# Rows of h computed during the last attention steps, and their six weights converted with fewer VectorE steps

## The chip, the cores and the metric

The kernel runs on one core of a Trainium2 chip. The metric is the device time of one launch in microseconds, the median of several runs.

## The reference, cut to what matters

```python
# q, k, v: [2, 8, 768, 64]; proj: [64, 6]; all float32
q_bits = einsum(q, proj) > 0 ; k_bits = einsum(k, proj) > 0       # 6 bits each
mask   = q_bucket[..., :, None] == k_bucket[..., None, :]
scores = where(mask, q @ k.T / sqrt(64), -1e9)
attn   = softmax(scores); x = (attn @ v) -> [1536, 512]
h = max(x @ w1, x @ w2, x @ w3)            # w: [512, 768]
y = h @ w_out                              # [768, 512]
u = y @ w_in                               # [512, 2048]
out = (u * clip(u + 3, 0, 6) / 6) @ w_out2 # [2048, 512]
```

All products keep float32 accuracy: an operand is split into a rounded high part and a low part, and a product is made of three matmuls (high by high, high by low, low by high). The host passes the weights as one int64 tensor of 56 blocks of 128 x 512 (`wts`), and the core turns each block back into a high and a low tile.

## The kernel before

The order of every engine is written out by hand (`tc.manual_schedule()`): an engine's queue holds instructions in the order in which the Python code issues them, and numbers at the top of the file say at which step a piece is issued.

**Attention** (`attention`, L237) has 16 heads in 8 pairs `p`. A prologue (`prologue`, L624) loads and splits the first pair, computes the bucket bits of head 0 (`bits_mm`, `bits_cmp`) and runs the six row-maximum units of head 0 (`max_unit`, L494 on TensorE, L498 on VectorE). Bits of the pair's second head go through a tile `bt` (`bits_bt`, L393) and two DMAs into the operand tiles (`bits_out`). Then 96 steps follow, six to a head, and six more (`LAG`) that only finish. In step `s` the program issues:

1. the product with V of step `s - 6` (`pv`, L578 to L584: 18 + 2 short matmuls), into the one PSUM buffer `x` of three steps; the division `norm` (L590, L595, L598: VectorE, tiles `xd`, `xr`, `xo`) must have read `x` before the next three steps write it;
2. the scores (`scores`, L544, four matmuls into one of two buffers `s`), and on ScalarE two exponentials of them, `E` (L548) and, in 16 bits, `ph` (L551); in some steps VectorE makes `ph` from `E` instead (L561; `PH_DVE`, and `PH_TAIL` from step `TAIL` on);
3. the low part `pl` (L566) of the step before, on GpSimd or, where `PL_DVE` or `PL_TAIL` says so, on VectorE;
4. a row-maximum unit for a step ten ahead (`mu`), and the tasks set for this step with `at` and `po`: loads, splits, bits of a later pair (`bits`, 12 matmuls), `vabs` to `vmean` for V, `fin` (L606, L607: transposes of the result, copied to `xF`), and the split of `x` of the first batch (`xhi` L199 on ScalarE, `xlo` L202 on VectorE, at the steps `XH`).

Three PSUM buffers with the tag `m` serve row maxima, bits, `fin`, `vsum` and `vmean` in turn.

**Weights** come by `job(i)` (L140), a generator that `tick` advances. It loads a block (`wraw`, 512 KB), scales half of it on ScalarE into `wy` (L146), takes three bits of the other half (`wr`: on VectorE for the first six blocks, L149; on GpSimd later, L155), joins them with two VectorE instructions (L160, L163), and writes the high tile `wh` on ScalarE (L169) and the low one `wl` on GpSimd (L171). In the attention `tick` is called after each step from `JS + 1` on, and starts jobs `JG` (in the tail `JT`) ticks apart, six in all (`J0`).

**The rows of h** (`hunit(ft, b, ..)`, L209) for a column tile `ft` (of 6) and a batch `b` (of 2) take 72 matmuls of 128 x 384: three weights by four blocks of x by three products by two halves (`mm`, L108). The unit (0, 0) is a generator `hu`: from step `HU0 = 92` on, each step issues six of its matmuls, and the rest goes between the last `fin` tasks. The other eleven units follow in `moe` (L764) one after the other, (1, 0) first; then come `w_out`, `w_in`, the gate and `w_out2`. `moe` splits x of the second batch at its start (`xsplit`, L205), while (1, 0) runs. Tiles that `moe` uses lie in memory that the attention has given up; the unit (0, 0) uses tiles `T` of the attention that are free by then.

## Time and profile before

| | us |
|---|---|
| median of 3 runs (lowest to highest) | 721.07 (720.88 to 722.88) |
| the profiled execution | 721.92 |
| span of the profiled execution, first to last instruction | 720.1 |
| TensorE matmul busy / weight load busy | 695.7 / 645.0 |
| VectorE / GpSimd / ScalarE busy | 456.7 / 395.6 / 337.0 |

The page has the busy time of each engine, the span in 40 slices (busy share in tenths, and the TensorE clock that was granted), and the chain of work that ended last. That chain is TensorE for 80% of the span and VectorE for 14%. Steps 0 to 95 can be told apart in the timeline by the first score matmul of each (L544, `s<-QB,KB`): step 0 begins at 18.1 us, step 12 at 58.6, step 72 at 192.3, step 88 at 228.9, step 95 at 246.0. `moe` begins at 263.3 us with (1, 0), and (0, 1) follows at 275.8.

### The profile page before, as it was taken

How to read it: one execution, taken by the hardware profiler on the slowest of the kernel's cores; microseconds unless marked ns; L12 is line 12 of the kernel's file. 1: busy time of each engine (PE TensorE's matmuls, PEld its weight loads, DVE VectorE, ACT ScalarE, POOL GpSimd, SP SyncE). 2: the span in 40 equal slices, each digit the busy share in tenths (PEclk: the TensorE clock that was granted, in tenths of full speed). 3: DMA queues.
4: the chain of work that ended last, by engine and by line, in shares of the span. 5: the costliest groups of instructions: out<-in, count | busy, mean ns of one | idle time of the engine just before them, and what ended most of it. 6: DMA issues, size and time to landing. Idle time of an engine off the chain costs nothing.

```text
span 720.1 us, 13570 instructions
## 1 busy us (share of the span) xinstructions
PE 695.7 (97%) x5343; PEld 645.0 (90%) x5343; DVE 456.7 (63%) x848; ACT 337.0 (47%) x564; POOL 395.6 (55%) x290
## 2 busy tenths in 40 slices
...
GB/s 179 108 163 125 110 190 139 116 163 169 107 121 56 35 59 60 88 88 89 30 59 89 60 30 58 59 87 64 115 66 80 92 26 62 86 30 1 1 77 99
DMA packets 22528, 61.82 MB, mean 86 GB/s; under 512 B 3864, under 2 KB 4952, under 8 KB 22464
## 3 DMA queue, kind: packets, MB, share of 16 engines
...
q8 instruction: 42, 0.69, 0.4%
...
q14 instruction: 22, 0.18, 0.1%
...
## 4 chain that ended last, share of the span: by engine, by line
PE 80%; DVE 14%; ACT 3%; issue 2%; DMA 1%; SPq 1%; DVEq 0%; ACTq 0%
PE s L108 28%; PE m L108 25%; PE s L544 7%; PE x L108 7%; PE m L494 4%; DVE mx L498 2%; PE x L578 2%; DVE G L788 2%; PE x L579 2%; PE x L580 2%; DVE wy L160 1%; DVE wy L163 1%; DVE pl L566 1%; DVE g L791 1%; ACT gr L782 1%
## 5 line engine op out<-in xcount | busy, mean ns | idle before, releaser
L155 POOL TENSOR_SCALAR wr<-wraw 128x256 int32<-128x256 uint32 x100 | 127.0, 1270 | 139.1 <-DVE wy L160 103.3
L566 POOL TENSOR_TENSOR pl<-E,ph 128x768 f16<-128x768 f32 x83 | 150.1, 1820 | 38.6 <-ACT ph L551 18.3
L498 DVE TENSOR_REDUCE mx<-m 128x1 f32<-128x384 f32 x192 | 97.0, 547 | 23.1 <-PE m L494 21.0
L548 ACT ACTIVATE E<-s 128x768 f32<-128x768 f32 x96 | 77.8, 810 | 55.9 <-PE s L544 47.2
L171 POOL TENSOR_TENSOR wl<-wy,wh 128x512 fp32r<-128x512 f32 x48 | 74.2, 1546 | 45.2 <-ACT wh L169 42.7
L108 PE MATMUL s<-G,wh 128*128 128x384 f32 x360 | 76.9, 334 | 0.0
L788 DVE TENSOR_TENSOR G<-g,G 128x384 fp32r<-128x384 f32 x56 | 45.0, 845 | 49.9 <-ACT G L787 49.4
L578 PEld LDWEIGHTS <-ph 128*128 128x128 f16 x576 | 54.8, 99 | 21.0 <-DVE xo L598 11.2
L578 PE MATMUL x<-VV,ph 128*128 128x65 f16 x576 | 65.8, 197 | 7.4 <-DVE xo L598 7.2
L169 ACT ACTIVATE wh<-wy 128x512 fp32r<-128x512 f32 x48 | 30.3, 631 | 75.5 <-DVE wy L163 75.5
L494 PE MATMUL m<-T,T 76*128 76x384 f32 x192 | 56.4, 366 | 9.5 <-DVE mx L498 4.6
L579 PE MATMUL x<-VV,ph 128*128 128x65 f16 x576 | 65.3, 197 | 0.0
L580 PE MATMUL x<-VV,pl 128*128 128x65 f16 x576 | 64.9, 194 | 0.0
L551 ACT ACTIVATE ph<-s 128x768 f16<-128x768 f32 x79 | 63.8, 808 | 0.0
L108 PEld LDWEIGHTS s<-G,wh 128*128 128x128 f32 x360 | 63.7, 188 | 0.0
L544 PE MATMUL s<-QB,KB 128*128 128x384 f32 x192 | 59.2, 391 | 0.8 <-ACT ph L551 0.8
L160 DVE SCALAR_TENSOR_TENSOR wy<-wy,wr 128x512 int32<-128x512 int32 x56 | 43.5, 778 | 25.1 <-POOL wr L155 25.0
L146 ACT ACTIVATE wy<-wraw 128x512 f32<-128x512 f32 x56 | 37.7, 672 | 45.5 <-POOL wl L171 27.5
L108 PE MATMUL m<-T,wh 128*128 128x384 f32 x240 | 58.6, 337 | 0.0
L579 PEld LDWEIGHTS <-ph 128*128 128x128 f16 x576 | 55.2, 99 | 0.6 <-issue 0.6
L108 PE MATMUL m<-G,wh 128*128 128x384 f32 x216 | 55.8, 334 | 0.0
L163 DVE SCALAR_TENSOR_TENSOR wy<-wraw,wy 128x512 int32<-128x512 int32 x56 | 54.3, 970 | 1.9
(209 smaller groups left out, 1682.5 us busy)
## 6 DMA issues: line engine op xcount, KB each, us to landing
...
```

Of the source, the lines that this page charges most:

```text
L108: pe.matmul(u[0:m, 0:n], l, r[:, hf * n:(hf + 1) * n], start=(first and i == 0), stop=(last and i == len(pairs) - 1),)
L155: pool.tensor_scalar(out=r3[:, c], in0=raw[:, c, 0].bitcast(U32), scalar1=2.0 ** -29, scalar2=7.0, op0=ALU.mult, op1=ALU.min,)
L171: pool.tensor_tensor(out=wl, in0=f32(y), in1=f32(wh), op=ALU.subtract)
L494: pe.matmul(u[:, 0:HF], QA[h % NA][0:76, qt * 128:qt * 128 + 128], KA[h % NA][0:76, hsl(hf)], start=True, stop=True,)
L498: dve.tensor_reduce(out=mx[h][:, qt, hf:hf + 1], in_=u[:, 0:HF], axis=AX.X, op=ALU.max)
L544: pe.matmul(u[:, k, 0:HF], a[0:n, c], b[0:n, hsl(hf)], start=n == 128, stop=n < 128)
L548: act.activation(out=e, in_=u[:, :, 0:HF], func=AF.Exp, scale=BIG)
L551: act.activation(out=ph.rearrange("p (a b) -> p a b", a=2), in_=u[:, :, 0:HF], func=AF.Exp, scale=BIG,)
L566: eng.tensor_tensor(out=pl, in0=e, in1=ph, op=ALU.subtract)
L578: pe.matmul(o, ph[:, c], vv[:, 0:65], start=kt == 0, stop=False)
L579: pe.matmul(o, ph[:, c], vv[:, 65:130], start=False, stop=False)
L580: pe.matmul(o, pl[:, c], vv[:, 0:65], start=False, stop=False)
```

## The change

- **h.** The units (0, 0) and (1, 0) are both issued in the attention, by a new generator `hfill`: per weight and half 12 matmuls into one `m` buffer, three of them to a call of `next` (48 calls in all). From step 88 on, each step makes two calls (six matmuls); six calls go ahead of each `fin` that is left after the last step, and two remain for the end. The running maximum goes to two new tiles `hF`, and `hsplit` splits them in `moe`, which starts with (0, 1).
- **x of the first batch** is split earlier, at steps 40, 49, 61, 69 (before: 81, 86, 89, 92), into tiles of its own.
- **The six early weights** start at steps 39, 45, 51, 57, 63, 69 (before: 63, 72, 81, 90, 94, 98). ScalarE, not VectorE, now makes `wr`, and the scaled half lies in a PSUM buffer `m` (`y0`), not in `wy`, until the two VectorE instructions have joined the parts.
- **Bits** of the second head (`bits_bt`, `bits_out`) are issued ahead of head 0's maxima. Numbers that place other tasks change too: row maxima of heads 1 and 2 (`MU`), loads into `KB` and `QB` (`AL`), `vabs`, `vmean`, the first `fin` of a pair; `TAIL` is 88, and in the tail ScalarE makes `ph` in three of six steps (before: in one). The prologue's warm-up matmuls are fewer, and the first six steps get some (`WS`).

```diff
-WARM = (9, 4, 4, 2)
-TAIL = 85
+WARM = (9, 4, 3, 1)
+TAIL = 88
+B0 = 0
+F0 = 2
+WS = (4, 0, 4, 2, 2, 2)
-PH_TAIL = (1, 2, 3, 4, 5)
+PH_TAIL = (1, 4, 3, 4, 3)
-MU = (0, 1, 1, 1, 2, 2, 4, 4, 5, 5, 6, 7)
+MU = (0, 1, 2, 2, 2, 2, 3, 4, 5, 6, 7, 7)
-AL = (-7, -5)
-VA, VS, VC, VH, VL, VE = -7, -6, (-6, -6, -6, -2), -2, -1, 3
+AL = (-9, -6)
+VA, VS, VC, VH, VL, VE = -9, -6, (-6, -6, -6, -2), -2, -1, 2
-FN = (26, 32)
-XH = (81, 86, 89, 92)
-HU0 = 92
-HUN = 6
-JS = 62
-JG = 9
+FN = (29, 32)
+XH = (40, 49, 61, 69)
+HU0 = 70
+HUN = 0
+HUT = 2
+HUE = 6
+JS = 38
+JG = 6
+JY = (2, 1, 2, 3)
...
     def job(i):
...
-        act.activation(out=f32(y), in_=f32(raw[:, :, 1]), func=AF.Copy, scale=2.0 ** -112)
+        y0 = unit("m") if early and JP else f32(y)
+        act.activation(out=y0, in_=f32(raw[:, :, 1]), func=AF.Copy, scale=2.0 ** -112)
...
-        if i < NW0:
-            dve.tensor_scalar(
-                out=r3, in0=raw[:, :, 0], scalar1=29, scalar2=None, op0=ALU.logical_shift_right
-            )
+                act.activation(
+                    out=r3, in_=raw[:, :, 0].bitcast(U32), func=AF.Copy,
+                    scale=2.0 ** -29 * (1 - 2.0 ** -20), bias=-0.5,
+                )
...
         dve.scalar_tensor_tensor(
-            out=y, in0=y, scalar=3, in1=r3, op0=ALU.logical_shift_left, op1=ALU.bitwise_or
+            out=y0, in0=y0, scalar=3, in1=r3, op0=ALU.logical_shift_left, op1=ALU.bitwise_or
         )
         dve.scalar_tensor_tensor(
-            out=y, in0=raw[:, :, 1], scalar=-2147483648, in1=y,
+            out=y, in0=raw[:, :, 1], scalar=-2147483648, in1=y0,
...
+    def hfill(ft):
+        for m in range(3):
+            wh, wl = weight(3 * ft + m, False)
+            for hf in range(2):
+                u, o = unit("m")[:, 0:HF], hF[ft][:, hsl(hf)]
+                for k in range(4):
+                    a, c = xS[0, k]
+                    w = slice(128 * k, 128 * k + 128)
+                    for i, (l, r) in enumerate(((wh, a), (wh, c), (wl, a))):
+                        pe.matmul(
+                            u, l[:, w], r[:, hsl(hf)], start=k == 0 and i == 0,
+                            stop=k == 3 and i == 2,
+                        )
+                    if k == 3 and m == 0:
+                        act.activation(out=o, in_=u, func=AF.Copy)
+                    elif k == 3:
+                        dve.tensor_tensor(out=o, in0=u, in1=o, op=ALU.max)
+                    yield
...
-            po(s, xhi, 0, k, T[k + 1], T[k + 6])
-            po(s + 1, xlo, 0, k, T[k + 1], T[k + 6])
-        hu = hunit(0, 0, T[0], T[5], "mm")
+            po(s, xhi, 0, k, xh0[k], xl0[k])
+            po(s + 1, xlo, 0, k, xh0[k], xl0[k])
+        hu = (None for f in range(2) for _ in hfill(f))
...
+            if s < LAG:
+                warm(WS[s])
             if s > JS:
                 tick(1, JG if s < TAIL else JT, J0)
             if s >= HU0:
-                next(hu, None)
+                for _ in range(HUN if s < TAIL else HUT):
+                    next(hu, None)
...
-        seq = [(1, 0), (0, 1), (1, 1)] + [(f, b) for f in range(2, 6) for b in range(2)]
+        for f in range(2):
+            hsplit(f, free.pop(0), free.pop(0))
+        seq = [(0, 1), (1, 1)] + [(f, b) for f in range(2, 6) for b in range(2)]
```

How the change moves instructions, at three places. First VectorE's queue in the prologue, from the last comparison of head 0's bits (`T<-s,pr`) on; `mx` are row maxima, `mr` and `mf` what is made of them. Before:

```order
L393 TENSOR_SCALAR T_94<-s,pr 12x384
L498 TENSOR_REDUCE mx<-m 128x1 x6
L505 TENSOR_REDUCE mq<-mx 128x3
L498 TENSOR_REDUCE mx<-m 128x1 x2
L517 TENSOR_SCALAR mr<-m 3x128
L518 SCALAR_TENSOR_TENSOR mr<-m,mr 3x128
L523 TENSOR_SCALAR mf<-m 3x128
L393 TENSOR_SCALAR bt<-s,pr 128x384 x2
L498 TENSOR_REDUCE mx<-m 128x1 x4
```

and with the change:

```order
L445 TENSOR_SCALAR T_91<-s,pr 12x384
L445 TENSOR_SCALAR bt<-s,pr 128x384 x2
L550 TENSOR_REDUCE mx<-m 128x1 x6
L557 TENSOR_REDUCE mq<-mx 128x3
L569 TENSOR_SCALAR mr<-m 3x128
L570 SCALAR_TENSOR_TENSOR mr<-m,mr 3x128
L575 TENSOR_SCALAR mf<-m 3x128
L550 TENSOR_REDUCE mx<-m 128x1 x6
```

The two `bt` instructions moved ahead of all maxima; on the DMA queue (SP) the two transfers `T<-bt` moved ahead of `T<-mr` likewise.

Second, VectorE's queue about steps 91 to 95; `xd`, `xr`, `xo` are one division, `T<-xF,T` an `xlo`, `wr` and `wy` a weight job. Before:

```order
L561 CAST ph<-E 128x768
L566 TENSOR_TENSOR pl<-E,ph 128x768
L149 TENSOR_SCALAR wr<-wraw 128x512
L561 CAST ph<-E 128x768
L202 TENSOR_TENSOR T_98<-xF,T_93 128x768
L160 SCALAR_TENSOR_TENSOR wy<-wy,wr 128x512
L163 SCALAR_TENSOR_TENSOR wy<-wraw,wy 128x512
L561 CAST ph<-E 128x768
L566 TENSOR_TENSOR pl<-E,ph 128x768
L590 TENSOR_SCALAR xd<-x,up 128x3
L595 RECIPROCAL xr<-xd 128x3
L598 TENSOR_TENSOR xo<-x,xr 128x3x64
```

and with the change:

```order
L613 CAST ph<-E 128x768
L618 TENSOR_TENSOR pl<-E,ph 128x768
L251 TENSOR_TENSOR hF_105<-m,hF_105 128x384
L613 CAST ph<-E 128x768
L618 TENSOR_TENSOR pl<-E,ph 128x768
L642 TENSOR_SCALAR xd<-x,up 128x3
L647 RECIPROCAL xr<-xd 128x3
L650 TENSOR_TENSOR xo<-x,xr 128x3x64
```

The weight job and the `xlo` are gone from here, and one maximum of h has come in.

Third, TensorE's queue at the end of the attention; `ident,xo` are the transposes of `fin`. Before, the last rows of (0, 0) and the first of (1, 0):

```order
L108 MATMUL m<-T_93,wh_104 128x384 x2
L108 MATMUL m<-T_98,wh_104 128x384 x2
L108 MATMUL m<-T_93,wl_105 128x384 x2
L606 MATMUL m<-ident,xo 128x128 x9
L108 MATMUL s<-T_90,wh_106 128x384 x2
L108 MATMUL s<-T_95,wh_106 128x384 x2
```

and with the change, the last rows of (1, 0):

```order
L244 MATMUL m<-xl_102,wh_117 128x384
L244 MATMUL m<-xh_98,wl_118 128x384
L658 MATMUL m<-ident,xo 128x128 x3
L244 MATMUL m<-xh_99,wh_117 128x384
L244 MATMUL m<-xl_103,wh_117 128x384
L244 MATMUL m<-xh_99,wl_118 128x384
L244 MATMUL m<-xh_100,wh_117 128x384
L244 MATMUL m<-xl_104,wh_117 128x384
L244 MATMUL m<-xh_100,wl_118 128x384
```

The transposes of the three last `fin` stood together; now 18 matmuls of h stand ahead of each, and six behind the last one.

## Rows read from the trace of the kernel before

**Rows 1.** Busy time by stage; the clock granted to TensorE is PEclk:

```profile
core 0: us, PE busy (x) PEld busy (x) DVE busy (x) ACT busy (x) POOL busy (x), PEclk, DMA share, GB/s
18.10:58.60 40.50, 34.71 (x265) 29.69 (x264) 29.91 (x71) 20.89 (x29) 23.41 (x14) 0.79 0.48 124
...
138.20:164.70 26.50, 25.71 (x351) 23.11 (x347) 22.81 (x56) 20.72 (x31) 22.12 (x14) 1.00 0.56 142
164.70:192.30 27.60, 26.50 (x352) 23.17 (x348) 24.54 (x59) 21.78 (x33) 22.64 (x15) 1.00 0.58 154
192.30:218.00 25.70, 23.50 (x339) 21.21 (x336) 23.72 (x58) 21.94 (x33) 23.21 (x16) 0.99 0.45 111
218.00:228.90 10.90, 8.83 (x119) 7.89 (x117) 10.69 (x20) 5.86 (x10) 4.38 (x4) 0.87 0.01 2
228.90:246.00 17.10, 15.14 (x197) 13.64 (x193) 15.61 (x22) 9.51 (x13) 10.58 (x6) 0.90 0.18 64
246.00:263.30 17.30, 16.23 (x195) 14.69 (x191) 12.77 (x24) 4.73 (x9) 5.14 (x3) 1.00 0.26 81
...
275.80:716.90 441.10, 439.89 (x2366) 416.53 (x2364) 230.48 (x345) 150.97 (x297) 201.85 (x148) 1.00 0.19 65
```

**Rows 2.** Waits of TensorE from 192.3 to 263.3 us: total, times, longest:

```profile
PE x L578 <- DVE xo L598: 6.6, 4, 2.1
```

**Rows 3.** Timeline about 221 us (start, duration): POOL, DVE, PE:

```profile
221.32 1.65 POOL L566 TENSOR_TENSOR pl<-E,ph 128x768 f16<-128x768 f32 x1 [1.85 <-issue]
...
221.48 2.03 DVE L160 SCALAR_TENSOR_TENSOR wy<-wy,wr 128x512 int32<-128x512 int32 x1
223.55 0.69 DVE L163 SCALAR_TENSOR_TENSOR wy<-wraw,wy 128x512 int32<-128x512 int32 x1
...
226.16 0.20 PE L578 MATMUL x<-VV,ph 128*128 128x65 f16 x1 [2.07 <-DVE xo L598]
```

**Rows 4.** The chain that ended last: 12 matmuls of bits, 24 of h:

```profile
160.97 2.16 PE m L108 x12
...
267.73 4.16 PE m L108 x24
```

**Rows 5.** Timeline of PE: scores of steps 93 and 94, h in steps 96 and 97:

```profile
241.01 0.59 PE L544 MATMUL s<-QB,KB 128*128 128x384 f32 x2
...
243.49 0.60 PE L544 MATMUL s<-QB,KB 128*128 128x384 f32 x2
...
248.44 0.94 PE L108 MATMUL m<-T,wh 128*128 128x384 f32 x4
...
250.20 0.95 PE L108 MATMUL m<-T,wh 128*128 128x384 f32 x4
```

**Rows 6.** Timeline of the start: DVE, SP's queue, PE:

```profile
15.78 1.12 DVE L393 TENSOR_SCALAR bt<-s,pr 128x384 fp32r<-128x384 f32 x2
...
17.80 1.57 SPq L103 DMA_DIRECT2D T<-bt  x2
...
21.02 0.98 PE L494 MATMUL m<-T,T 76*128 76x384 f32 x2 [2.01 <-DMA T<-bt]
...
42.44 0.44 PE L494 MATMUL m<-T,T 76*128 76x384 f32 x1 [2.39 <-DVE mx L498]
```

**Rows 7.** DVE's timeline, and ACT's scaling of the weights (min/median/max ns):

```profile
177.52 1.60 DVE L149 TENSOR_SCALAR wr<-wraw 128x512 int32<-128x512 int32 x1
...
217.95 2.34 DVE L465 SCALAR_TENSOR_TENSOR VV<-xF,up,VV 128x768 f16<-128x768 f32 x1
...
228.75 0.94 DVE L202 TENSOR_TENSOR T<-xF,T 128x768 fp32r<-128x768 f32 x1
...
L146 ACT ACTIVATE wy<-wraw x11: 662/669/712, 177.0 to 295.9; 128x512 f32<-128x512 f32 x11
```

**Rows 8.** Waits from 100 to 200 us: total, times, longest:

```profile
ACT kH L322 <- DMA KB<-kH: 3.7, 4, 1.7
...
PE s L544 <- ACT ph L551: 0.8, 3, 0.3
```

More of the change, by code (lines that the diff above doesn't have):

```diff
@@ L36 @@
 PL_HEAD = (8,)
-PH_TAIL = (1, 2, 3, 4, 5)
+PH_TAIL = (1, 4, 3, 4, 3)
 PL_TAIL = (1, 3, 5)
-MU = (0, 1, 1, 1, 2, 2, 4, 4, 5, 5, 6, 7)
+MU = (0, 1, 2, 2, 2, 2, 3, 4, 5, 6, 7, 7)
 E1 = (0, 1, (1, 1, 1, 1), 2)
-E2 = (1, 0, 2)
-E3 = (0, 1)
+E2 = (0, 0, 2)
+E3 = (0, 2)
 E5 = 4
-E4 = ((0, 0), (2, 4), (3, 5))
-LQK, LV = -23, -22
+E4 = ((0, 0), (2, 4), (3, 7))
+LQK, LV = -25, -22
 L2 = (3, 4)
@@ L126, in body @@
     xF = big.tile([128, NP, S], F32, name="xF")
+    xh0 = [big.tile([128, S], F32R, name=f"xh{i}") for i in range(4)]
+    xl0 = [big.tile([128, S], F32R, name=f"xl{i}") for i in range(4)]
+    hF = [big.tile([128, S], F32, name=f"hF{i}") for i in range(2)]
     Wsl = [
@@ L142, in job @@
         sp.dma_start(out=raw, in_=wts[i].bitcast(I32).rearrange("p (n t) -> p n t", t=2))
-        yield
-        yield
+        early = i < NW0
+        for _ in range(JY[0] if early else 2):
+            yield
         y = o2.tile([128, 512], I32, name="wy")
-        act.activation(out=f32(y), in_=f32(raw[:, :, 1]), func=AF.Copy, scale=2.0 ** -112)
+        y0 = unit("m") if early and JP else f32(y)
+        act.activation(out=y0, in_=f32(raw[:, :, 1]), func=AF.Copy, scale=2.0 ** -112)
+        y0 = y0.bitcast(I32)
         r3 = o1.tile([128, 512], I32, name="wr")
-        if i < NW0:
-            dve.tensor_scalar(
-                out=r3, in0=raw[:, :, 0], scalar1=29, scalar2=None, op0=ALU.logical_shift_right
-            )
-            yield
+        if early:
+            if JR:
+                dve.tensor_scalar(
+                    out=r3, in0=raw[:, :, 0], scalar1=29, scalar2=None,
+                    op0=ALU.logical_shift_right,
+                )
+            else:
+                act.activation(
+                    out=r3, in_=raw[:, :, 0].bitcast(U32), func=AF.Copy,
+                    scale=2.0 ** -29 * (1 - 2.0 ** -20), bias=-0.5,
+                )
+            for _ in range(JY[1]):
+                yield
         else:
@@ L160, in job @@
         dve.scalar_tensor_tensor(
-            out=y, in0=y, scalar=3, in1=r3, op0=ALU.logical_shift_left, op1=ALU.bitwise_or
+            out=y0, in0=y0, scalar=3, in1=r3, op0=ALU.logical_shift_left, op1=ALU.bitwise_or
         )
         dve.scalar_tensor_tensor(
-            out=y, in0=raw[:, :, 1], scalar=-2147483648, in1=y,
+            out=y, in0=raw[:, :, 1], scalar=-2147483648, in1=y0,
             op0=ALU.bitwise_and, op1=ALU.bitwise_or,
         )
-        yield
+        for _ in range(JY[2] if early else 1):
+            yield
         wh, wl = held[i]
         act.activation(out=wh, in_=f32(y), func=AF.Copy)
-        yield
+        for _ in range(JY[3] if early else 1):
+            yield
         pool.tensor_tensor(out=wl, in0=f32(y), in1=f32(wh), op=ALU.subtract)
@@ L193, in weight @@
         return held[i]
+    mp = {}
     xS = {}
@@ L207, in xsplit, with hsplit @@
         xlo(*a)
+    def hfill(ft):
[10 more added lines that the diff above has]
+                            stop=k == 3 and i == 2,
+                        )
+                    if k == 3 and m == 0:
+                        act.activation(out=o, in_=u, func=AF.Copy)
+                    elif k == 3:
+                        dve.tensor_tensor(out=o, in0=u, in1=o, op=ALU.max)
+                    yield
+    def hsplit(ft, hi, lo):
+        for hf in range(2):
+            c = hsl(hf)
+            act.activation(out=hi[:, c], in_=hF[ft][:, c], func=AF.Copy)
+            dve.tensor_tensor(out=lo[:, c], in0=hF[ft][:, c], in1=f32(hi[:, c]), op=ALU.subtract)
+        hT[ft, 0] = (hi, lo)
     def hunit(ft, b, hh, hl, tags=None):
```

43 lines of the change are left out of this document (23 added, 20 removed).

## The prediction

> **What bounds the kernel now.** I read the busy time by stage first [rows 1]. From 275.8 us to the end TensorE is busy 439.9 of 441.1 us: nothing in that stretch can be gained except by giving TensorE less to do there. The two middle stages (12 steps each) have TensorE busy 25.7 of 26.5 and 26.5 of 27.6 us at full clock, so the attention is TensorE's too, with VectorE (22.8 of 26.5) and ScalarE (20.7) close behind. The end of the attention is another matter: from 192.3 to 263.3 us TensorE is idle 7.3 us in sum (the spans of the four stages less their busy times), and its clock is granted at 0.87 and 0.90 from 218.0 to 246.0, while VectorE is busy 10.69 of 10.9 us there. The start, 18.1 to 58.6 us, has 5.8 us of idle TensorE and a clock of 0.79.
>
> Next the waits. In the end of the attention TensorE waits for one thing, the division `xo` that frees the buffer `x`: 6.6 us in four waits [rows 2]. The timeline shows why [rows 3]: a joining instruction `wy` sits in VectorE's queue for 2.03 us, one of its kind takes 0.69 right after, and `xo` stands behind it; TensorE then waits 2.07 us. So the weight jobs and the x splits, put late, hold the division up.
>
> **The change part by part.** The sum is made against the profiled execution, whose span is 720.1 us and whose own time, 721.92, is 0.85 above the median of the runs, 721.07; the differences below are taken off the median.
>
> *Moved rows of h.* 72 matmuls leave the stretch after 263.3 us. Twenty-four of them take 4.16 us there [rows 4], so 12.5 us go, and they come back in the attention. What counts is how long the attention then is, so I go by stages.
>
> *Steps 72 to 87* (36.6 us now, 192.3 to 228.9). The jobs after the first, and the four `xlo`, leave this stretch. I take the middle stage without a job, 26.5 us [rows 1], less the 12 matmuls of bits, 2.2 [rows 4], which no pair needs any more: 24.3 for steps 72 to 83. For 84 to 87: a step with six matmuls of h is 2.47 us from score to score [rows 5], those six are 1.04 [rows 4], so a bare step is 1.43; four of them, two last maxima (0.7, at some 0.17 us a matmul as in [rows 4]) and about 0.9 for `vmean`, are 7.3. Sum 31.6, a gain of 5.0. Between 3 (half the stalls stay) and 6.
>
> *Steps 88 to 94* (17.1 us). Each now has six matmuls of h, where before only those from 92 on had: 7 x 2.47 = 17.3, a loss of 0.2. The waits on `xo` that filled the early steps are replaced by work. Between -1 and +2; VectorE has `ph` in three of six steps, not in five, so it is not what I expect to bound.
>
> *From step 95 to unit (0, 1)* (29.8 us, 246.0 to 275.8). Rest of step 95: 1.8. Six steps with `pv` and six matmuls: 248.44 to 250.20 is 1.76 [rows 5], so 10.6. Then 60 matmuls, 10.4, and four sets of transposes at about 0.3, 1.2. After the last transposes the copy to `xF` and the four splits of the second batch can no longer hide behind (1, 0), only behind six matmuls. One copy, one `xhi` and one `xlo` (0.94, [rows 7]) follow each other, and the product needs the low part third of six matmuls; I take a wait of 1.1, bounds 0.3 and 3. Sum 25.1, a gain of 4.7.
>
> *The middle, steps 40 to 74.* It gains six jobs (before: one) and four splits. VectorE: the two joining instructions at 0.69 [rows 3] are 1.4 a job, 8.3 in all; `wr` (up to 1.60, [rows 7]) is no longer its work; four `xlo` at 0.94, or up to the 2.34 that an instruction of that width with two SBUF operands took [rows 7], are 3.8 to 9.4. Together 12.1 to 17.7 us, where VectorE idles 3.7 us in 26.5, some 10 us over the stretch. ScalarE: scaling and the new `wr` at 0.67 each [rows 7] (same shape, so the same price for `wr`), `wh` as before, four `xhi`: about 15 us into some 16 idle. Neither fits without friction. The price of it is read from the first job: the stage with it is 27.6, the one without 26.5 [rows 1], 1.1 us of span for some 3 us of VectorE (1.60 and two joining instructions of at least 0.69), about a third. A third of 13 is 4.4. Against that, the first job's own 1.1 leaves, and the loads of `KB` issued earlier (`AL`) end ScalarE's waits for them before `kH` (3.7 us in four, [rows 8]), of which TensorE saw less than a microsecond a wait: 1.0 off. Net a loss of 2.3, between -2 (new work all in idle time) and +7 (a third of 17.7, and one `m` buffer in three held by `y0` for a step, which no row shows). The 512 KB loads move ahead with the jobs and stand directly ahead of `mr` on SP's queue, as the first job's did; that one held no score up, so I put it at nothing. If that cover goes, a score waits for `mr`, at a price that D below bounds.
>
> The Trainium skill, page "SBUF — State Buffer", section "Who interferes with whom", has a rule for both kinds: a VectorE instruction with two SBUF inputs and a GpSimd instruction that reads SBUF block each other whole, one with at most one SBUF input outside the 2-port modes does not. The timeline agrees [rows 3] (2.03 beside the 1.65 of `pl`, 0.69 after it). By it the first joining instruction, with one input now in PSUM, always takes its short time, and the `xlo`, moved to where GpSimd is busy 22.1 of 26.5 us, would mostly take the long one, so the middle would cost nearer 5 than 2.3.
>
> *The start.* `bt` is made at 15.78 and its transfers are issued at 17.80, and TensorE waits 2.01 us for them [rows 6]; made five microseconds earlier, they are landed before step 0 ends. That wait goes; next late is `qL` of pair 1. The other long wait, 2.39 behind two instructions of `vmean` on VectorE, loses half by fewer maxima behind it: 1.2. Gain 3.2, between 0 and 6. I count nothing for the clock, which is a rival below.
>
> *Rest of the kernel.* `moe` needs weights 6 to 8 at 25 us after its start, not 37; a job is passed through six ticks, two to each 4.16 us, so weight 6 is there after about 19. Nothing.
>
> Sum: -5.0 + 0.2 - 4.7 + 2.3 - 3.2 = **-10.4 us, so 710.7 us**.
>
> **The rivals.**
>
> *A. The middle fills up.* VectorE or ScalarE becomes the bound in steps 40 to 74, and the `xlo` queue behind GpSimd. For it: the sums above just reach the idle time. Against: lags of one step are absorbed, since maxima run ten steps ahead. Then the middle costs 7: 715.4 us.
>
> *B. The clock at the start holds.* The stage up to 58.6 us has 34.7 us of busy TensorE at 0.79; at full clock that is 7.3 less. For it: the waits that come before the fall go, and warm-up matmuls stand in the first steps. Against: most of those steps wait for chains of VectorE, ScalarE and DMA and not for TensorE. 703.4 us.
>
> *C. The filler does not fit.* TensorE waits as before in the tail, say for the maxima of h or for weights 3 to 5, and the 72 matmuls lengthen the attention by what they leave. Then only start and middle count, -0.9: 720.2 us.
>
> *D. Slower: `y0` and the pair on ScalarE stall the steps.* Each early job puts 1.3 us of ScalarE ahead of an `E`, and holds one of three `m` buffers until VectorE, itself late, has joined the parts; row maxima then run in lockstep with VectorE and the step waits. Decisive from where a job costs TensorE more than about 2.1 us (12.7, the sum without the middle, by six). At a lost step and a half, 2.8 us: 721.07 - 12.7 + 16.8 = 725.2 us. Against: the first job, with more VectorE work, cost 1.1.
>
> **How the numbers follow.** Chances: forecast 0.56, A 0.20, B 0.13, C 0.06, D 0.05. About 0.3% (2.2 us) can be told from no change. Forecast, A and B lie below 718.9: faster 0.89. C is no change, 0.06; D slower, 0.05. The forecast's own bounds, not all at their ends at once, are 705 to 715; to reach 8 in 10 I take in A and the near half of B: 703.5 to 716.5.
>
> **What would show it.** The division's waits before `pv` from step 80 on gone, and the clock at 1.0 from 218 us on; step 88 about 6 us earlier counted from step 72; `moe` starting with (0, 1) some 10 us before 275.8, after a wait of about a microsecond for the split. In the middle, 12 steps of 27 to 28.5 us; more would be A or D (told apart by `E` waiting for nothing but ScalarE, or maxima waiting for a buffer). No wait for `T<-bt` at step 0. Wrong is the forecast if the attention's end stays put while `moe` is 12.5 us shorter only on paper, or if the gain comes from the start.

## The result, and the profile after

| | before | changed |
|---|---|---|
| median of 4 runs each (us) | 721.87 | 704.07 |
| lowest to highest | 720.88 to 722.88 | 703.10 to 706.24 |
| profiled execution / its span | 721.92 / 720.1 | 703.10 / 701.3 |

The ratio is 0.9757, with a 95% interval of 0.9727 to 0.9788. The medians differ by 17.8 us (2.5%), where 10.4 were forecast. A fourth run of the kernel before moved its median from 721.07 to 721.87; the forecast of 710.7 was taken off the former. The time lies at the lower end of the range, near rival B.

The stages between the first scores of steps are cut in the same places as in [rows 1]. Busy time by stage of the changed kernel; columns as in [rows 1]:

```profile
17.80:51.60 33.80, 31.28 (x294) 26.36 (x293) 29.63 (x71) 21.80 (x31) 24.26 (x14) 1.00 0.62 162
51.60:102.00 50.40, 50.25 (x691) 45.60 (x688) 43.86 (x111) 40.36 (x58) 44.57 (x28) 1.00 0.58 151
102.00:128.20 26.20, 25.64 (x352) 23.11 (x349) 23.91 (x59) 22.59 (x34) 22.58 (x15) 1.00 0.68 180
128.20:155.10 26.90, 26.07 (x354) 23.25 (x350) 25.17 (x61) 24.07 (x38) 25.45 (x17) 1.00 0.68 175
155.10:183.10 28.00, 26.38 (x353) 23.23 (x349) 26.34 (x62) 25.72 (x40) 26.57 (x17) 1.00 0.60 157
183.10:213.70 30.60, 30.23 (x452) 27.52 (x449) 26.19 (x67) 25.66 (x38) 27.55 (x21) 1.00 0.28 60
213.70:231.60 17.90, 17.90 (x223) 16.78 (x219) 6.52 (x13) 10.69 (x16) 8.14 (x5) 1.00 0.17 61
231.60:256.20 24.60, 24.32 (x244) 22.95 (x241) 7.76 (x18) 5.26 (x10) 4.42 (x3) 1.00 0.01 1
256.20:697.70 441.50, 439.89 (x2363) 416.42 (x2364) 234.59 (x349) 154.83 (x303) 202.04 (x148) 1.00 0.19 64
```

The rows are steps 0 to 11, 12 to 35, 36 to 47, 48 to 59, 60 to 71, 72 to 87, 88 to 94, from step 95 to the unit (0, 1), and (0, 1) onward. TensorE idled 7.3 us from step 72 to 263.3 us before; now it idles 0.4 us in steps 72 to 87, none in 88 to 94 and 0.3 in what follows. The granted clock is 1.00 in each row of this execution, the fastest of the four, where [rows 1] has 0.79 at the start and 0.87 and 0.90 late in the attention. VectorE, 15.61 us busy in steps 88 to 94 before, is busy 6.52. What has become full is steps 60 to 71: VectorE 26.34 of 28.00 us. From (0, 1) on, the rows are as before (439.89 us of TensorE in both).

The waits of TensorE in the changed kernel from 50 to 257 us (total, times, longest) are short, and the 6.6 us of [rows 2] are 0.6:

```profile
PE m L475 <- DVE mx L550: 1.4, 3, 0.5
...
PE m L546 <- DVE bt L445: 0.8, 1, 0.8
...
PE x L630 <- DVE xo L650: 0.6, 3, 0.3
...
PE s L115 <- ACT G L224: 0.3, 1, 0.3
```

Where the 18.8 us of span came from, by the same cuts, against the terms of the sum:

| stretch | before | after | difference | forecast |
|---|---|---|---|---|
| start, up to step 12 | 58.6 | 51.6 | -7.0 | -3.2 |
| steps 12 to 35 | 52.4 | 50.4 | -2.0 | 0 |
| steps 36 to 71 | 81.3 | 81.1 | -0.2 | +2.3 |
| steps 72 to 87 | 36.6 | 30.6 | -6.0 | -5.0 |
| steps 88 to 94 | 17.1 | 17.9 | +0.8 | +0.2 |
| step 95 to (0, 1) | 29.8 | 24.6 | -5.2 | -4.7 |
| (0, 1) to the end | 444.3 | 445.1 | +0.8 | 0 |

Three terms held within about a microsecond. The start gave twice its term, and the steps between 12 and 72 gave 4.5 us more than forecast. The experiments are about these two, about what in the change makes the middle cheap, and about what the moved rows of h are worth.

### The profile page after: what moved, and what is told of

It reads as the page before. It is cut to its first block, busy times and chain, and to the rows that moved or that the text cites. A ratio compares the mean times of both kernels' runs of the same rounds, so it can differ in the third digit from the quotient of the medians.

```text
span 701.3 us, 13612 instructions
## 1 busy us (share of the span) xinstructions
PE 686.9 (98%) x5363; PEld 638.3 (91%) x5363; DVE 436.3 (62%) x834; ACT 343.2 (49%) x576; POOL 396.7 (57%) x292
## 4 chain that ended last, share of the span: by engine, by line
PE 65%; DVE 6%; ACT 2%; issue 1%; DVEq 0%
PE s L115 28%; PE m L115 21%; PE x L115 7%; PE m L244 4%; PE s L596 2%; DVE T L846 1%; ACT gr L840 1%; DVE g L849 1%; DVE wy L185 1%; PE x L630 1%; PE x L631 1%; DVE G L846 1%; PE x L632 1%; DVE wy L182 1%; DVE mx L550 1%
## 5 line engine op out<-in xcount | busy, mean ns | idle before, releaser
L618 POOL TENSOR_TENSOR pl<-E,ph 128x768 f16<-128x768 f32 x85 | 152.4, 1807 | 29.5 <-ACT ph L603 15.8
L600 ACT ACTIVATE E<-s 128x768 f32<-128x768 f32 x96 | 78.1, 813 | 37.4 <-PE s L596 29.5
L603 ACT ACTIVATE ph<-s 128x768 f16<-128x768 f32 x85 | 68.9, 810 | 0.0
L630 PE MATMUL x<-VV,ph 128*128 128x65 f16 x576 | 64.2, 195 | 1.3 <-DVE xo L650 0.6
L631 PE MATMUL x<-VV,ph 128*128 128x65 f16 x576 | 63.8, 195 | 0.0
L115 PE MATMUL m<-G,wh 128*128 128x384 f32 x252 | 63.0, 334 | 0.0
L158 ACT ACTIVATE wy<-wraw 128x512 f32<-128x512 f32 x50 | 33.6, 673 | 50.3 <-POOL wl L195 32.1
L115 PE MATMUL s<-G,wh 128*128 128x384 f32 x264 | 56.8, 335 | 0.9 <-DVE G L227 0.6
L846 DVE TENSOR_TENSOR T<-g,T 128x384 fp32r<-128x384 f32 x40 | 29.8, 786 | 42.9 <-ACT T L845 42.9
L632 PEld LDWEIGHTS <-pl 128*128 128x128 f16 x576 | 54.6, 99 | 0.0
L182 DVE SCALAR_TENSOR_TENSOR wy<-wy,wr 128x512 int32<-128x512 int32 x50 | 37.5, 751 | 25.4 <-POOL wr L177 25.4
L185 DVE SCALAR_TENSOR_TENSOR wy<-wraw,wy 128x512 int32<-128x512 int32 x50 | 50.1, 1003 | 1.7
L596 PE MATMUL s<-T,T 98*128 98x384 f32 x192 | 49.6, 340 | 0.2 <-DMA T<-mr 0.2
```

Source lines behind the costliest of these rows:

```text
L115: pe.matmul(u[0:m, 0:n], l, r[:, hf * n:(hf + 1) * n], start=(first and i == 0), stop=(last and i == len(pairs) - 1),)
L185: dve.scalar_tensor_tensor(out=y, in0=raw[:, :, 1], scalar=-2147483648, in1=y0, op0=ALU.bitwise_and, op1=ALU.bitwise_or,)
L596: pe.matmul(u[:, k, 0:HF], a[0:n, c], b[0:n, hsl(hf)], start=n == 128, stop=n < 128)
L600: act.activation(out=e, in_=u[:, :, 0:HF], func=AF.Exp, scale=BIG)
L603: act.activation(out=ph.rearrange("p (a b) -> p a b", a=2), in_=u[:, :, 0:HF], func=AF.Exp, scale=BIG,)
L618: eng.tensor_tensor(out=pl, in0=e, in1=ph, op=ALU.subtract)
```

## The experiments

One letter and number a run: e for the start, m for the middle, t for the tail, c for a combination. Differences in the text are between medians unless a profile is named. The changed kernel's median is 704.07. The kernel before was run again beside each group of runs, with medians from 720.7 to 721.9, so a difference of about a microsecond between runs of different groups can't be told from none. Durations of stages, in us, are between the first scores of steps in each kernel's profile (step 0 begins at 17.8 to 19.6 us in all):

| kernel | 0-11 | 12-23 | 24-35 | 36-47 | 48-59 | 60-71 | 72-79 | 80-87 | 88-94 | 95-end | span | median | ratio to before (95%) |
|---|---|---|---|---|---|---|---|---|---|---|---|---|---|
| before | 40.6 | 26.2 | 26.2 | 27.1 | 26.5 | 27.6 | 16.6 | 20.1 | 17.0 | 474.1 | 720.1 | 721.87 | |
| changed | 33.8 | 25.1 | 25.3 | 26.2 | 26.9 | 28.0 | 15.9 | 14.7 | 17.9 | 469.7 | 701.3 | 704.07 | 0.9757 (0.9727-0.9788) |
| e1_start_old | 39.9 | 25.1 | 25.3 | 26.2 | 26.9 | 28.0 | 15.8 | 14.7 | 17.9 | 469.7 | 709.2 | 711.00 | 0.9858 (0.9822-0.9895) |
| e2_no_ws | 33.4 | 25.1 | 25.3 | 26.2 | 26.9 | 28.0 | 15.9 | 14.7 | 17.9 | 469.7 | 701.0 | 702.90 | 0.9751 (0.9716-0.9786) |
| e3_bits_ahead | 36.9 | 26.2 | 26.3 | 27.1 | 26.5 | 27.6 | 16.6 | 21.2 | 15.5 | 475.1 | 717.1 | 718.51 | 0.9959 (0.9936-0.9982) |
| e4_warm_only | 38.7 | 26.2 | 26.5 | 26.5 | 27.0 | 27.6 | 16.6 | 20.0 | 17.0 | 474.2 | 718.5 | 721.59 | 1.0015 (0.9994-1.0036) |
| m1_y0_sbuf | 34.1 | 25.1 | 25.3 | 26.5 | 31.6 | 32.7 | 17.7 | 14.8 | 17.9 | 469.7 | 713.1 | 715.15 | 0.9918 (0.9901-0.9936) |
| m2_wr_vector | 35.1 | 25.1 | 25.3 | 26.5 | 29.5 | 31.7 | 18.0 | 14.7 | 17.9 | 469.8 | 711.4 | 717.46 | 0.9946 (0.9924-0.9968) |
| m3_places_old | 32.9 | 26.2 | 26.8 | 27.0 | 28.4 | 28.9 | 16.6 | 15.3 | 17.6 | 469.8 | 707.3 | 710.24 | 0.9854 (0.9829-0.9879) |
| m4_jobs_late | 32.8 | 25.1 | 25.3 | 25.3 | 25.3 | 27.1 | 17.9 | 22.3 | 17.9 | 469.8 | 708.1 | 710.50 | 0.9858 (0.9833-0.9883) |
| m5_loads_old | 34.6 | 27.9 | 26.7 | 26.7 | 30.0 | 28.8 | 16.1 | 14.8 | 17.9 | 469.7 | 711.1 | 712.54 | 0.9877 (0.9846-0.9907) |
| t1_half_fill | 33.9 | 25.1 | 25.3 | 26.2 | 26.9 | 28.0 | 15.8 | 14.7 | 17.9 | 468.4 | 700.2 | 702.31 | 0.9740 (0.9716-0.9764) |
| t2_split_ahead | 34.9 | 25.1 | 25.3 | 26.2 | 26.9 | 28.0 | 15.8 | 14.8 | 17.9 | 468.2 | 701.1 | 702.46 | 0.9736 (0.9716-0.9755) |
| c1_spread | 33.0 | 30.2 | 26.0 | 26.8 | 28.5 | 27.4 | 15.6 | 14.8 | 17.9 | 468.4 | 706.5 | 709.00 | 0.9833 (0.9805-0.9860) |

### The start

**e1_start_old**: the changed kernel with all of the old start.

```diff
-WARM = (9, 4, 3, 1); B0 = 0; F0 = 2; WS = (4, 0, 4, 2, 2, 2)
+WARM = (9, 4, 4, 2); B0 = 4; F0 = 3; WS = (0, 0, 0, 0, 0, 0)
-MU = (0, 1, 2, 2, 2, 2, 3, 4, 5, 6, 7, 7)
+MU = (0, 1, 1, 1, 2, 2, 4, 4, 5, 5, 6, 7)
-E2 = (0, 0, 2); E3 = (0, 2); E4 = ((0, 0), (2, 4), (3, 7))
+E2 = (1, 0, 2); E3 = (0, 1); E4 = ((0, 0), (2, 4), (3, 5))
...
-                warm(WARM[2] if qt < 3 else WARM[3])
+                warm((4, 4, 4, 0, 2, 2)[qt])
```

> The changed kernel with the start of the kernel before: the order of bits, maxima, loads and warm-up matmuls up to step 12 goes back, all else stays. Theory: start and tail are separate terms, so the start's gain of 7.1 us (step 12 at 51.6 instead of 58.6 us) goes and nothing else, step 12 comes at about 58.5 us, the clock falls there again, and the median is near 711 us. Rival: much of the gain of steps 12 to 36 (2.0 us) comes from the start too (bits and loads that run later), then step 36 comes some 9 us later and the median is near 713.

Measured: 711.00, 6.9 us slower than the changed kernel. The row of the table differs from the changed kernel's in the first stage alone (by 0.1 us at most elsewhere; step 0 begins at 19.6 us here and at 17.8 there), so the start is a term of its own, worth about 7 us.

**e2_no_ws**: the changed kernel without the warm-up matmuls in the first six steps.

```diff
-WS = (4, 0, 4, 2, 2, 2)
+WS = (0, 0, 0, 0, 0, 0)
```

> The changed kernel without the 14 warm-up matmuls of steps 0 to 5. Theory W (the warm-up matmuls hold the clock): the clock of the start falls below 0.9 as before, step 12 comes 3 to 4 us later, the median is 707 to 708 us. Theory O (the order took the long waits away, and the clock stays up by that): the clock stays over 0.97, step 12 comes up to 1 us earlier since 14 matmuls of about 0.1 us are gone, the median is 703 to 704 us.

Measured: 702.90; with or without them the interval is nearly the same. The clock of steps 0 to 11 is 0.95, a little under the 0.97 that theory O asked for. The warm-ups are not what makes the start short.

**e3_bits_ahead**: the kernel before, with one part of the change, the bits of the second head ahead of head 0's maxima.

```diff
+            for hf, u in enumerate(us):
+                bits_bt(0, hf, u)
+            bits_out(0, 1)
             for qt in range(3):
...
-            for hf, u in enumerate(us):
-                bits_bt(0, hf, u)
-            bits_out(0, 1)
```

> The kernel before with one thing of the change: the bits of the second head and their transfers ahead of head 0's maxima. Theory O: the wait of 2.0 us for T<-bt goes, the clock after it stays up longer, step 12 comes 3 to 5 us earlier, the median is about 718 us. Theory W: only the wait goes, the clock of the stage to step 12 stays near 0.8, 1 to 2 us are gained, the median is about 720 us.

Measured: 718.51, 3.1 us below the kernel before in the runs beside it (ratio 0.9959). In the profiles step 12 comes 3.7 us earlier: TensorE idles 1.4 us less (5.8 to 4.4), and its 264 matmuls are busy 32.36 us, not 34.71 (265 matmuls), at a clock of 0.86 in place of 0.79. So the move alone gives about half of the start's 7 us. What gives the other half (the places of `max_fin`, `max_out`, the bits of pair 1 and the row maxima of the next heads, which go back together in e1) was not separated.

**e4_warm_only**: the kernel before, with the warm-ups of the first six steps alone.

```diff
+            if s < LAG:
+                warm((4, 0, 4, 2, 2, 2)[s])
```

> The kernel before with one other thing of the change: the 14 warm-up matmuls behind steps 0, 2, 3, 4 and 5. Theory W: the clock of the start rises over 0.9 and step 12 comes 2 to 4 us earlier. Theory O: the wait of 2.0 us at step 0 stands ahead of the warm-up matmuls, the clock falls after it as before, and step 12 comes between 0.5 us earlier and 1.5 us later.

Measured: 721.59, no change (ratio 0.9994 to 1.0036). Its profile has step 12 come 1.8 us earlier than before, more than theory O allowed, but that execution is the fastest of the ten. Steps 0 to 11 of the four kernels, in the order e1, e2, e3, e4 (columns as in [rows 1]):

```profile
19.60:59.50 39.90, 33.62 (x265) 28.66 (x265) 29.87 (x71) 20.65 (x29) 21.67 (x13) 0.83 0.53 143
```

```profile
17.90:51.30 33.40, 29.66 (x267) 24.81 (x265) 29.98 (x71) 21.54 (x30) 23.93 (x14) 0.95 0.64 163
```

```profile
18.10:54.90 36.80, 32.36 (x264) 27.22 (x264) 29.95 (x71) 21.23 (x29) 23.81 (x14) 0.86 0.54 135
```

```profile
18.20:56.90 38.70, 35.20 (x295) 30.25 (x293) 29.00 (x71) 21.44 (x30) 23.48 (x14) 0.87 0.51 130
```

With the old order the clock is 0.83 (e1, no warm-ups in these steps; 0.79 in the kernel before) or 0.87 (e4, with them); with the new order it is 0.95 without any. From e1 to e2, both without warm-ups in the steps and with as many matmuls, idle TensorE goes from 6.3 to 3.7 us and busy TensorE from 33.62 to 29.66. So the order does both: it takes idle time away and, with it, most of the time at the lower clock.

The clock of 1.00 in the changed kernel's profile is not fixed by that order. The runs m1, m2, m4, t1 and t2 below have the same instructions in steps 0 to 11, and their profiles show 0.95, 0.90, 0.95, 0.95 and 0.90 there. The stage takes them 32.8 to 35.1 us, against 38.7 to 40.6 with the old order.

### The middle: how a weight job is made

**m1_y0_sbuf**: the scaled half of a weight lies in `wy` (SBUF) again, not in a PSUM buffer `m`.

```diff
-JP = 1
+JP = 0
```

> The changed kernel with the scaled half of the six early weights in SBUF (wy), not in a PSUM buffer m. Theory: the first joining instruction then has two SBUF inputs and waits in some of the six for GpSimd, as in the kernel before (2.03 and 2.15 us in two of six); 2 to 5 us of VectorE more in steps 40 to 74, a third of that in the span: 1 to 2 us slower. Rival: holding one of three m buffers is the larger price (the waits of 0.5 us at vsum in steps 42, 54 and 66); then the three waits go and the span is 0.5 to 1.5 us shorter.

Measured: 715.15, 11.1 us slower; the direction was expected, the size far from it. First VectorE and GpSimd in the changed kernel at one of its jobs, and two of its `xlo`, from the timeline (start, duration):

```profile
134.87 0.95 DVE L227 TENSOR_TENSOR xl<-xF,xh 128x768 fp32r<-128x768 f32 x1
...
169.43 3.25 POOL L618 TENSOR_TENSOR pl<-E,ph 128x768 f16<-128x768 f32 x2
...
170.25 0.68 DVE L182 SCALAR_TENSOR_TENSOR m<-m,wr 128x512 int32<-128x512 int32 x1
171.02 0.69 DVE L185 SCALAR_TENSOR_TENSOR wy<-wraw,m 128x512 int32<-128x512 int32 x1
...
179.44 1.42 DVE L227 TENSOR_TENSOR xl<-xF,xh 128x768 fp32r<-128x768 f32 x1
```

and the same in m1, with an `xlo` behind it:

```profile
132.23 3.89 POOL L618 TENSOR_TENSOR pl<-E,ph 128x768 f16<-128x768 f32 x2 [0.22 <-ACT ph L603]
...
131.35 1.21 DVE L182 SCALAR_TENSOR_TENSOR wy<-wy,wr 128x512 int32<-128x512 int32 x1
132.59 2.02 DVE L185 SCALAR_TENSOR_TENSOR wy<-wraw,wy 128x512 int32<-128x512 int32 x1
137.32 2.71 DVE L227 TENSOR_TENSOR xl<-xF,xh 128x768 fp32r<-128x768 f32 x1
```

In the changed kernel both joins take their short time beside GpSimd's `pl`, all six times:

```profile
L182 DVE SCALAR_TENSOR_TENSOR m<-m,wr x6: 680/680/689, 116.3 to 185.3; 128x512 int32<-128x512 int32 x6
...
L185 DVE SCALAR_TENSOR_TENSOR wy<-wraw,m x6: 686/688/690, 117.1 to 186.1; 128x512 int32<-128x512 int32 x6
```

(minimum, median and maximum in ns). In m1 the first joins take 0.69 to 1.21, five of the six second joins 2.02 to 2.03, and two `xlo` 2.70 and 2.71. In steps 48 to 71 VectorE is busy 9.6 us more than in the changed kernel (61.12 against 51.51), and the span pays nearly all of it (9.4). VectorE is then 95% busy, and TensorE waits for its maxima. Steps 48 to 59 and 60 to 71 of m1, and TensorE's wait for a maximum from 128 to 194 us:

```profile
128.80:160.40 31.60, 27.11 (x353) 23.30 (x349) 29.96 (x61) 24.46 (x38) 26.61 (x17) 1.00 0.61 156
160.40:193.10 32.70, 28.26 (x351) 24.64 (x347) 31.16 (x62) 25.99 (x40) 27.52 (x17) 0.95 0.50 126
```

```profile
PE m L546 <- DVE mx L550: 5.3, 4, 1.7
```

The rival, that holding an `m` buffer for `y0` costs more than the long joins, falls: giving the buffer back loses 11 us.

**m2_wr_vector**: VectorE makes `wr` again, not ScalarE.

```diff
-JR = 0
+JR = 1
```

> The changed kernel with wr of the six early weights on VectorE again. Theory (VectorE bounds the middle): six instructions of 0.4 to 1.6 us more on VectorE, each stage of twelve steps 0.5 to 1 us longer, the whole 2 us slower. Rival (ScalarE bounds it, being busy 24.1 and 25.7 us of 26.9 and 28.0): taking 4 us from ScalarE wins, the whole is 1 to 2 us faster.

Measured: 717.46 (713.17 to 719.88 in nine runs; the profiled run is the fastest, so the stages in the table show less than the median does). VectorE in its timeline, two `wr` and an `xlo`:

```profile
131.45 1.87 DVE L164 TENSOR_SCALAR wr<-wraw 128x512 int32<-128x512 int32 x1
...
145.21 0.42 DVE L164 TENSOR_SCALAR wr<-wraw 128x512 int32<-128x512 int32 x1
...
167.83 2.82 DVE L227 TENSOR_TENSOR xl<-xF,xh 128x768 fp32r<-128x768 f32 x1
```

Three of the six `wr` take 0.42 us and three, beside a `pl` of GpSimd, 1.87; one `xlo` takes 2.82. VectorE is busy 6.4 us more in steps 48 to 71, and these steps are 6.3 us longer. So an instruction that can take 0.42 us cost the kernel over 10 us for six, in the queue that bounds these steps. The direction was expected, the size far from it. On ScalarE the same work takes 0.67 (after, the same view as above for the joins):

```profile
L169 ACT ACTIVATE wr<-wraw x6: 667/671/696, 115.3 to 183.3; 128x512 int32<-128x512 uint32 x6
```

### The middle: where tasks stand

**m3_places_old**: the old places of `KB` and `QB` loads, `vabs`, `vmean` and `fin`.

```diff
-AL = (-9, -6); VA = -9; VE = 2; FN = (29, 32)
+AL = (-7, -5); VA = -7; VE = 3; FN = (26, 32)
```

> The changed kernel with the old places of the loads into KB and QB (AL), of vabs and vmean and of the first fin. Theory: these places, and not the start, gave the 2.0 us of steps 12 to 36 and hide about as much of the jobs' price in steps 36 to 72; the stage of steps 12 to 36 goes from 50.4 to 52.5 us, ScalarE waits for KB<-kH again, the stages of steps 36 to 72 go up by 2 to 4 us, and the median is 4 to 6 us higher. Rival: they matter little with the start in order; within 1 us.

Measured: 710.24, 6.2 us slower. Each 12 steps from 12 to 72 cost 0.8 to 1.5 us more, and steps 72 to 87 cost 1.3. So a few numbers that place tasks, of which the forecast credited one with 1.0 us, give about 6.

**m5_loads_old**: of these, the loads alone.

```diff
-AL = (-9, -6)
+AL = (-7, -5)
```

> The changed kernel with only the loads into KB and QB (AL) at their old places; vabs, vmean and the first fin stay at the new ones. All four old places together cost 6.2 us of the median and made each stage of twelve steps 0.8 to 1.5 us longer. Theory L (the loads: the split kH waits on ScalarE for KB<-kH of the pair before, and the exponentials behind it with it): most of it comes back, 0.7 to 1.3 us a stage, the median near 708 to 709 us, and ScalarE's waits for KB<-kH are back. Rival V (vabs, vmean and fin did it): under 0.4 us a stage, the median under 706 us.

Measured: 712.54, 8.5 us slower. The intervals of its ratio and of m3's overlap, so that it is slower than m3 is not shown; but the loads alone cost about as much as all four old places. Theory L holds in kind, with a larger price than expected. The waits of ScalarE in m5 from 78 to 196 us:

```profile
ACT kH L374 <- DMA KB<-kH: 2.7, 3, 1.3
ACT kH L374 <- DMA QB<-qL: 2.5, 1, 2.5
```

The first is that of [rows 8]; in the changed kernel ScalarE waits for no DMA in these steps. The forecast knew these waits and took TensorE's share of each as less than a microsecond. Steps 12 to 23 and 48 to 59 of m5, which lose the most (2.8 and 3.1 us):

```profile
52.40:80.30 27.90, 26.74 (x345) 24.12 (x342) 22.04 (x56) 19.83 (x28) 22.45 (x14) 0.94 0.55 140
133.70:163.80 30.10, 27.83 (x354) 24.75 (x350) 26.36 (x61) 24.12 (x38) 26.11 (x17) 0.94 0.61 164
```

Here the clock is 0.94, where the changed kernel and m3 have 1.00. Over steps 12 to 71 TensorE idles 7.7 us in m5 and 3.2 in the changed kernel, and with about as many matmuls is busy 132.5 us and 128.3: half of the loss is waiting, half matmuls at a lower clock. The six jobs, which stand in the same queues, can't be the whole reason, since 4.2 us of the loss lie in steps 12 to 35, ahead of the first job. Why the clock falls in these two stages, and not in m3, is not shown. Some other numbers of the change were taken back by no run, `LQK` (when a pair's `q` and `k` are loaded), `JY` (the ticks between the parts of a job), `TAIL` and `PH_TAIL` among them.

**m4_jobs_late**: the jobs and the splits of x back to the end of the attention (the rows of h stay).

```diff
-XH = (40, 49, 61, 69); JS = 38; JG = 6
+XH = (72, 76, 80, 84); JS = 62; JG = 5
```

> The changed kernel with the six weight jobs at steps 63 to 88 and the four x splits at 72 to 84, about where the kernel before had them; the filler stays. Theory (lateness was the loss): steps 36 to 72 get 3 to 5 us shorter, steps 72 to 95 get 5 to 8 us longer by waits for the division behind joins and splits, the whole is 1 to 4 us slower. Rival (the joins through PSUM and the wr on ScalarE are what made it good, the place counts for little): steps 72 to 95 get at most as much longer as 36 to 72 get shorter, the whole is within 1 us or faster.

Measured: 710.50, 6.4 us slower, more than the 1 to 4 expected. Steps 36 to 71 are 3.4 us shorter, and 72 to 87 are 9.6 longer: steps 80 to 87 take 22.3 us, where the clock falls:

```profile
198.10:220.40 22.30, 17.52 (x220) 14.94 (x219) 18.96 (x40) 16.34 (x26) 13.99 (x11) 0.85 0.10 30
220.40:238.30 17.90, 17.90 (x222) 16.79 (x219) 9.55 (x15) 12.74 (x20) 10.63 (x7) 1.00 0.26 90
```

with a row maximum waiting for a buffer that a job holds, in TensorE's timeline:

```profile
208.31 1.16 PE L546 MATMUL m<-T,T 76*128 76x384 f32 x2 [3.15 <-DVE wy L185]
```

Steps 88 to 94 (the second row) are as in the changed kernel. So the gain of steps 72 to 87 is the early place of jobs and splits. Twelve steps without a job take 25.3 us with the new places (36 to 59 here). The jobs and splits therefore cost the changed kernel 26.2 + 26.9 + 28.0 - 3 x 25.3 = 5.2 us, where 4.4 was put down.

### The tail

**t1_half_fill**: only (0, 0) is issued in the attention; (1, 0) goes back to `moe`, ahead of (0, 1).

```diff
-        hu = (None for f in range(2) for _ in hfill(f))
+        hu = (None for f in range(1) for _ in hfill(f))
...
-        seq = [(0, 1), (1, 1)] + [(f, b) for f in range(2, 6) for b in range(2)]
+        seq = [(1, 0), (0, 1), (1, 1)] + [(f, b) for f in range(2, 6) for b in range(2)]
```

> The changed kernel with only the unit (0, 0) as filler; (1, 0) goes back to the start of what follows, in full. Theory (the filler's second half fills idle time of TensorE): without it TensorE waits in the last steps and between the last transposes, and of the 12.5 us that go back only a part is saved in the attention; 2 to 4 us slower. Rival (with jobs and splits gone from the tail, TensorE has no idle time there to fill): the attention gets 10 to 12 us shorter, the wait of 0.9 us for the split goes behind (1, 0), and the whole is within 1 us of the changed kernel.

Measured: 702.31, no worse than the changed kernel, and 1.3 us less in its profile from step 95 to the end. From step 95 to 258.0 us its TensorE has no gap:

```profile
231.80:258.00 26.20, 26.20 (x255) 25.21 (x252) 13.07 (x26) 9.54 (x18) 4.42 (x3) 1.00 0.01 1
```

Moving (1, 0) into the attention is worth nothing by itself: with the jobs and splits gone there is no idle time left for it to fill, and without (1, 0) at the start of `moe` the splits of the second batch lose their cover.

**t2_split_ahead**: the changed kernel with three of these splits issued ahead of the last two `fin`.

```diff
+                    if (a[0], a[1]) == (7, 0):
+                        xsplit(1, 0, T[1], T[6])
+                        xsplit(1, 1, T[2], T[7])
+                    if (a[0], a[1]) == (7, 1):
+                        xsplit(1, 2, T[3], T[8])
...
-        for k in range(4):
-            xsplit(1, k, G[10 + 2 * k], G[11 + 2 * k])
-        free = T + G[18:]
+        xsplit(1, 3, G[10], G[11])
+        free = [T[0], T[4], T[5], T[9]] + G[12:]
```

> The changed kernel with the splits of the second batch's first three blocks issued between the last fin tasks, into tiles T that are free by then. Theory: the two waits at the start of (0, 1), 0.28 and 0.61 us, and part of the start of the splits go, and (0, 1) begins some 0.9 to 1.2 us earlier; the median is about 1 us lower. Rival: ScalarE and VectorE then hold up the copies and maxima of the filler, and nothing is gained.

Measured: 702.46, 1.5 us less from step 95 to the end. The waits that it takes away, in the changed kernel's timeline at the start of (0, 1):

```profile
256.20 0.62 PE L115 MATMUL s<-G,wh 128*128 128x384 f32 x2 [0.28 <-ACT G L224]
...
257.43 0.62 PE L115 MATMUL s<-G,wh 128*128 128x384 f32 x2 [0.61 <-DVE G L227]
```

t1 and t2 have the lowest medians seen. Their intervals overlap the changed kernel's, so that they beat it is not shown.

### A wider spread

**c1_spread**: t1, without the warm-ups of the first six steps, and the jobs started at steps 18, 27, and so on to 63.

```diff
-JS = 38; JG = 6
+JS = 17; JG = 9
```

> The changed kernel with three things that the other runs point to: no warm-up matmuls in steps 0 to 5, the unit (1, 0) back at the start of what follows, and the six weight jobs spread wider, at steps 18 to 63, nine apart. Theory: the price of a job grows with the jobs in a stage (one in twelve steps costs 0.5 us, two with a split or two 1.6 to 2.7), so spread they cost 3 to 4 us in all in place of 5.2; with the other two the median is 700 to 701.5 us. Rival: the price is the sum of VectorE's work wherever it stands, or DMA loads of 512 KB collide with those of the pairs; then no more than the other two give, 702 us or above.

Measured: 709.00, slower than t1 by 6.7 us; the expectation was missed. Steps 60 to 71 are 0.6 us shorter than in t1, but steps 48 to 59 are 1.6 longer and steps 12 to 23 are 5.1 longer. Steps 12 to 23 and 24 to 35 of c1, and TensorE's longest wait in the first of them:

```profile
50.90:81.10 30.20, 27.51 (x346) 24.97 (x342) 24.89 (x58) 20.85 (x31) 21.45 (x14) 0.89 0.55 145
81.10:107.10 26.00, 25.45 (x352) 23.08 (x349) 23.03 (x58) 22.40 (x35) 23.74 (x16) 1.00 0.65 163
```

```profile
70.78 0.44 PE L546 MATMUL m<-T,T 76*128 76x384 f32 x1 [1.58 <-DVE mf L575]
```

VectorE has 5 us to spare in that stage, so its sum does not explain it. Half of the 5.1 us is the clock again: at 0.89 the 346 matmuls are busy 27.51 us, where the changed kernel's 347 take 25.00 at 1.00. The other half is waiting. The trace has one job here, and its `y0` holds an `m` buffer for 6.5 us (68.84 to 75.34), where the six of the changed kernel hold theirs for 3.0 to 4.1; the bits of a later pair wait 1.00 us for it. Whether that hold, the job's place in VectorE's queue or its load is the cause, no run separates; the step at which a job falls matters more here than how many fall into a stretch.

## Why the prediction was right, and where not

- **What bounds the attention's end, and what moving the jobs gives: right.** The division's waits fell from 6.6 us to 0.6, the clock is 1.00 there, and steps 72 to 87 gave 6.0 where 5.0 was worked out. With the old places (m3) they take 16.6 + 15.3 = 31.9 us, and the forecast's sum was 31.6; the last microsecond is the places'. m4 shows that it is the jobs and splits.
- **Steps 88 to 94 and the rest up to (0, 1): right.** 17.9 against 17.3 us, all of it busy; 24.6 against 25.1, with 0.28 of the wait for the splits of batch two ahead of (0, 1) and 0.61 behind its first matmuls (1.1 had been put down). But the step "72 matmuls leave" carries no gain of its own: t1 leaves 72 of them in `moe` and is as fast.
- **The middle: its price about right, the credit against it too small.** With the old places, steps 36 to 71 take 84.3 us (m3) against 81.3 before: +3.0, where 4.4 less the first job's 1.1 had been forecast. The step that failed is "1.0 off" for the loads issued earlier. The places are worth 3.2 us in these steps (84.3 to 81.1) and some 3 more in others, for which nothing had been counted; the loads alone, put back in m5, cost 4.4 in these steps and 4.2 in steps 12 to 35. The forecast read the four waits of ScalarE as mostly hidden, and left out that matmuls at a lower clock can follow on a wait. That the price came near is in part luck. "About a third" took 3 us of VectorE for the first job, but in [rows 1] VectorE is busy only 1.7 us more in the stage that has it (24.54 against 22.81); the measured rate is over a half, 5.2 us for 9.7 us more of VectorE (75.4 in steps 36 to 71, against 21.9 in each twelve steps of m4 without a job).
- **Joins and splits.** The forecast took 0.69 for both joins and 0.94 for `xlo`; measured are 0.68, 0.69 and, for `xlo`, 0.95 three times and 1.42 once. The Trainium skill, page "SBUF — State Buffer", section "Who interferes with whom", says that a VectorE instruction with at most one SBUF input, outside the 2-port modes, does not contend with GpSimd: the trace agrees for both joins (each now has one input in PSUM), and m1 shows the price of two SBUF inputs. From the rule's other half the prediction took that the `xlo` "would mostly take the long one". With these places three of four ran short: each starts at the end of a `pl` (0.13 us or less before it) or beside none, and only the fourth, begun 0.6 us before the end of a `pl`, takes 1.42.
- **The start: the mis-sized term.** 2.0 for the wait on `T<-bt` and 1.2 for `vmean`'s; bits ahead alone (e3) gave 3.7 in the profiles and 3.1 in the medians, and the whole start 7. "I count nothing for the clock" is the step that failed: between the two profiles idle TensorE went from 5.8 to 2.5 us and busy TensorE from 34.71 to 31.28, more matmuls included, at a clock of 0.79 and 1.00. Rival B was half right: the clock rises, to 0.90 to 1.00 from profile to profile, but by the order and not by the warm-ups it named beside it (e2, e4).
- **The other rivals.** A (VectorE the bound) shows in steps 60 to 71, 26.34 of 28.00 us busy, without the 7 us; it does come about as soon as a job costs VectorE more (m1, m2). C falls by the tail, D by the middle: the joins of five of the six jobs lie in steps 36 to 71, so a job costs 5.2 / 5, about a microsecond with its share of the splits, and not the 2.1 from which D decides.
- **The number: in part luck.** The forecast missed by 6.6 us (710.7 against 704.07), and the range, stretched to take in half of B, holds with 0.6 us to spare. That the time lies by B's 703.4 is chance: by B the start is 10.5 us shorter, and it was 7.0; steps 12 to 71 made up the rest. By its own last sign, "if the gain comes from the start", the forecast was in part wrong: 7.0 of the 18.8 us of span come from there.
